# Attention and two expert layers on one core: PSUM in one-bank tiles, the first pair's key-value group in two parts, first loads on two queues

## The chip, the cores and the metric

The kernel runs on one core of a Trainium2 chip. The metric is the device time of one execution in microseconds (us); the number that counts is the median over several executions. The core has TensorE (PE: matmuls, with weight loads shown apart as PEld), VectorE (DVE), ScalarE (ACT), GpSimd (POOL) and SyncE (SP, which here issues loads and stores). Each engine works through its own instructions in the order in which the program was written out, and waits where an instruction needs something that another engine hasn't delivered.

## The reference, cut to what matters

Three stages follow each other, all in float32:

```python
def phi(x):                                   # q, k: (4, 8, 576, 64), w_phi: (64, 128)
    proj = np.einsum('bhsd,df->bhsf', x, w_phi)
    proj = proj - np.max(np.abs(proj), axis=-1, keepdims=True)
    return np.concatenate([np.exp(proj), np.exp(-proj)], axis=-1)
q_p, k_p = (phi(q), phi(k))
kv = np.einsum('bhsf,bhsd->bhfd', k_p, v)
z = np.sum(k_p, axis=2)
num = np.einsum('bhsf,bhfd->bhsd', q_p, kv)
den = np.einsum('bhsf,bhf->bhs', q_p, z)[..., None] + 1e-06
x = num / den                                 # then 2304 tokens of 512 features
...
e_idx = np.argmax(x @ w_gate, axis=1)         # 8 experts, one for each token
h = np.maximum(x[mask] @ w1[e], 0.0)
out[mask] = gate_w[mask, None] * eom[mask, e, None] * (h @ w2[e])
...
xn = x / np.sqrt(np.mean(x * x, axis=-1, keepdims=True) + 1e-06) * rms_g
g = xn @ w_gate
return (g * (1.0 / (1.0 + np.exp(-g))) * (xn @ w_val)) @ w_out     # 512 -> 1536 -> 512
```

## The kernel before, in words

**Attention** (`attn`, L358) runs over four batches, and in each over four pairs of heads. Of the 576 rows of a head 512 are handled in four chunks of 128; the 64 left over of all eight heads are packed into one more pass, the leftovers `"L"`. For each of them a load (L367, L373) brings rows of `k` or `q`, PE transposes them (L400), ACT copies them (L403), PE projects them (L410) into a tile `pp` of two banks of PSUM, and DVE takes the maximum (L414) and subtracts it (L416), which gives `d`. For keys ACT makes the exponentials `e` (L465), PE multiplies them with `v` in groups of five matmuls for each head, four chunks and the leftovers (L474 to L480), and the result goes by way of `ks` (L481, L486) into `kv` (L490). For queries PE transposes `d`, ACT takes exponentials (L433), PE multiplies with `kv` (L533), DVE divides (L440 to L444) into `x`, PE transposes it, and ACT and DVE write it as two parts that add up to it (L545, L547) into `xh`.

**The first expert layer** (`gate`, L582, and `moe`, L698) follows for each batch. From the leftovers alone an expert is guessed for the whole batch (`guess`, L553), whose number, `star` (L576), is read by SP so that the expert's weights can be loaded early (L711); ACT and DVE split them into two parts (L712, L713). Then come sixteen groups of twelve matmuls for the first product (`mm1`, L682; each is read by ACT, L729, and DVE, L731, which write `h`) and eight groups of 24 for the second (`mm2`, L691; read by DVE, L743, into `y`). Tokens that would have needed another expert are handled by `general` (L899) afterwards.

**The second layer** (`unit`, L846) takes the tokens in six units of 384. In a unit, for each of twelve pieces of the hidden size, PE makes a gate and a value product (L860, twelve matmuls each, written out in two halves of six), ACT applies the activation to the first (L866), DVE multiplies it with the second (L868), ACT and DVE split the product in two parts (L870, L871), and PE multiplies them with the output weights (L878). The weights come in a packed form that ACT and DVE decode from `raw` (L776 to L789): half of the gate and value weights during the last expert stage, the rest during unit 0. The next unit's input is normalised (`prep`, L802) beside.

**The order** of all this is not written by hand. A planner (`Graph`, L42) keeps the ready tasks of each engine, gives each a cost (`dur`) and a priority, and writes out in each step the task that could start first by its own clock; tasks take buffers from slots with names (`pa`, `pp`, `ph`, `pgv`, `po`, `pms` for PSUM). The waits between engines are put in below the planner, by the tile: an instruction waits for those written out before it that used the same tile in a conflicting way.

**PSUM** has eight banks. `psum` (L299) makes one pool of two tiles of two banks, `pq0` and `pq1`, and four of one bank. The two-bank tiles serve the projections. After nine of them `pq1` leaves that duty (`halve`, L308) and its halves become two more slots `ph` for the experts' groups, three in all. In the second layer `pgv` is a one-bank tile, both halves of `pq1` and one half of `pq0`:

```python
        self.ps = one + [t[:, i] for t in self.two[::-1] for i in range(2)]
...
    g.slot("pgv", kk.ps[3:7])
```

## Time and profile before

| | |
|---|---|
| Time, median of 3 runs | 957.31 us (956.15 to 957.85) |
| The profiled execution: its own time | 959.13 us |
| Its span | 957.5 us, 14539 instructions |
| PE busy | 914.5 us (96%) |
| weight loads busy | 835.9 us (87%) |
| DVE busy | 433.9 us (45%) |
| ACT busy | 337.4 us (35%) |
| moved by DMA | 74.60 MB, mean 78 GB/s |

The stretches give the busy time of each engine in a part of the span and the clock that PE was granted, as a share of 2.4 GHz; the waits give the idle time of an engine by what ended it; the timeline has instructions in order of time, neighbours of one kind in one row, with the idle time of their engine ahead of them in brackets. A float32 matmul stands in the trace as two records in attention and as one in the expert layers. The batches of attention and of the first expert layer lie interleaved up to about 364 us, the last batch's expert stage fills the time up to 483, then come the border and unit 0 of the second layer (to about 576), and units 1 to 5.

### The profile page before, as it was taken

The page shows a single profiled execution, that of the slowest core. Times are in us where ns is not written, and L with a number is a line of the kernel's source. Part 1 is how long each engine was busy: PE and PEld are TensorE (multiplying, and loading weights), DVE is VectorE, ACT ScalarE, POOL GpSimd, SP SyncE. Part 2 cuts the span into 40 slices and gives each one's busy share as a digit, 9 for nine tenths or more (in the row PEclk, how much of TensorE's full clock was granted, in tenths as well). Part 3 has the DMA queues.
Part 4 walks back from the last instruction along what each step waited for, and adds up shares of the span by engine and source line. Part 5 has one row for each costly group of instructions (what it writes and reads, how often), then busy time and mean ns, then how long its engine had stood idle before and what let it go on. Part 6 is the DMA issues. An engine that isn't in the chain of part 4 may idle for free. (4 is left out here: it accounts for less than half of the span.)

```text
span 957.5 us, 14539 instructions
## 1 busy us (share of the span) xinstructions
PE 914.5 (96%) x6044; PEld 835.9 (87%) x6045; DVE 433.9 (45%) x826; ACT 337.4 (35%) x588; POOL 3.2 (0%) x23
## 2 busy tenths in 40 slices
PE   7988999999999998999989799999999999999998
PEld 5677799789889997898988789999999998999997
DVE  4454565556444547884248882322323133132111
ACT  4343435534433325543145551322223123122111
POOL 1000000000000000000000000000000000000000
PEclk9997999999999999999999989999999999999999
DMA  5313513421511146673145440002001002000000
GB/s 147 105 56 109 139 47 117 143 62 45 180 56 55 49 159 200 181 231 102 48 135 156 148 139 34 1 1 67 1 1 66 1 1 67 1 1 34 1 1 34
DMA packets 84984, 74.60 MB, mean 78 GB/s; under 512 B 30256, under 2 KB 78512, under 8 KB 84400
## 3 DMA queue, kind: packets, MB, share of 16 engines
q1 hardware_dynamic: 84912, 73.60, 25.2%
q8 instruction: 50, 0.82, 0.4%
q14 instruction: 22, 0.18, 0.1%
HBM read 54.63 MB, written 18.96 MB: 77 GB/s over the span
## 5 line engine op out<-in xcount | busy, mean ns | idle before, releaser
L860 PE MATMUL pq<-xn,wgv 128*128 128x384 f32 x1296 | 240.0, 338 | 12.3 <-DVE sil L868 12.3
L860 PEld LDWEIGHTS pq<-xn,wgv 128*128 128x128 f32 x1296 | 227.1, 189 | 18.5 <-DVE sil L868 9.2
L878 PE MATMUL ps<-wo,a 128*128 128x512 f32 x648 | 160.5, 392 | 0.0
L868 DVE TENSOR_TENSOR sil<-pq,sil 128x384 f32<-128x384 f32 x71 | 39.6, 557 | 223.9 <-PE pq L860 223.9
L878 PEld LDWEIGHTS ps<-wo,a 128*128 128x128 f32 x648 | 120.7, 188 | 22.0 <-DVE a L871 0.2
L860 PE MATMUL ps<-xn,wgv 128*128 128x384 f32 x432 | 81.2, 335 | 2.5 <-PEq L914 2.5
L860 PEld LDWEIGHTS ps<-xn,wgv 128*128 128x128 f32 x432 | 75.9, 188 | 5.3 <-issue 2.7
L682 PE MATMUL pq<-xh,w 128*128 128x288 f32 x492 | 73.3, 300 | 7.4 <-DVE h L731 7.1
L691 PE MATMUL pq<-h,w 128*128 128x288 f32 x528 | 76.5, 298 | 2.8 <-DVE y L743 2.2
L870 ACT CAST a<-sil 128x384 fp32r<-128x384 f32 x72 | 36.8, 512 | 118.7 <-DVE sil L868 118.7
L682 PEld LDWEIGHTS pq<-xh,w 128*128 128x128 f32 x492 | 66.4, 188 | 10.7 <-DVE h L731 7.5
L691 PEld LDWEIGHTS pq<-h,w 128*128 128x128 f32 x528 | 71.3, 188 | 4.4 <-DVE y L743 3.1
L209 PE MATMUL ps<-kv,qp 128*128 128x65 f32 x512 | 69.2, 276 | 5.7 <-DVE x L444 4.5
L209 PEld LDWEIGHTS ps<-kv,qp 128*128 128x128 f32 x512 | 67.6, 201 | 7.8 <-DVE x L444 4.9
L414 DVE TENSOR_REDUCE m<-pq 128x8 f32<-128x1024 f32 x36 | 43.9, 1223 | 49.6 <-PE pq L410 45.9
L209 PE MATMUL ps<-e,v 128*65 128x256 f32 x256 | 63.2, 389 | 0.7 <-ACT e L465 0.7
L871 DVE TENSOR_TENSOR a<-sil,a 128x384 fp32r<-128x384 f32 x72 | 39.9, 555 | 28.8 <-ACT a L870 28.4
L209 PEld LDWEIGHTS ps<-e,v 128*65 128x65 f32 x256 | 35.0, 142 | 19.3 <-issue 1.8
L712 ACT CAST w<-wr 128x1024 fp32r<-128x1024 f32 x32 | 33.5, 1047 | 45.6 <-PE pq L691 18.5
L713 DVE TENSOR_TENSOR w<-wr,w 128x1024 fp32r<-128x1024 f32 x32 | 39.2, 1224 | 20.5 <-ACT w L712 19.8
L866 ACT ACTIVATE sil<-ps 128x384 f32<-128x384 f32 x35 | 17.2, 491 | 85.6 <-PE ps L860 85.6
L433 ACT ACTIVATE qp<-ps 128x512 f32<-128x512 f32 x64 | 34.7, 598 | 33.6 <-PE ps L209 30.1
(141 smaller groups left out, 985.7 us busy)
## 6 DMA issues: line engine op xcount, KB each, us to landing
wr<-in_moe_w SPq DMA_DIRECT2D x32, 512.0 KB, 3.7
xdr<-xh SPq DMA_DIRECT2D x4, 2304.0 KB, 9.4
raw<-in_moe_w_gate SPq DMA_DIRECT2D x12, 512.0 KB, 3.5
raw<-in_moe_w_val SPq DMA_DIRECT2D x12, 512.0 KB, 4.2
raw<-in_moe_w_out SPq DMA_DIRECT2D x12, 512.0 KB, 3.7
yu<-ydr SPq DMA_DIRECT2D x6, 768.0 KB, 4.9
qk<-in_k SPq DMA_DIRECT2D x16, 256.0 KB, 3.5
v<-in_v SPq DMA_DIRECT2D x32, 128.0 KB, 2.6
```

The lines of the kernel that those rows point to most:

```text
L209: f()
L414: g.t("DVE", dve(1024), lambda: nc.vector.tensor_reduce(out=m.ap, in_=pv(), axis=AX.X, op=ALU.max, apply_absolute_value=True), r=[pp], w=[ ...
L433: g.t("ACT", act(512), lambda f=f: nc.scalar.activation(qp.ap[:, f].rearrange("p c t -> p (c t)"), pd.ap, AF.Exp, scale=1.0 - 2.0 * f), r= ...
L682: self.nc.tensor.matmul(ph[:, 0:HS], lhsT=wv[:, a, c, fs], rhs=xh[:, x, c, cs], start=(c == 0 and i == 0), stop=(c == NC - 1 and i == 2))
L691: self.nc.tensor.matmul(ph[:, 0:HS], lhsT=wv[:, a, f], rhs=hs[f][:, x, cs], start=(f == 0 and i == 0), stop=(f == 7 and i == 2))
L712: g.t("ACT", act(1024, False), lambda: nc.scalar.copy(w.ap[:, 0], wr.ap), r=[wr], w=[w], prio=pr - AHEAD)
L713: g.t("DVE", dve(1024), lambda: nc.vector.tensor_tensor(out=w.ap[:, 1], in0=wr.ap, in1=w.ap[:, 0], op=ALU.subtract), r=[wr], rw=[w], prio= ...
L860: nc.tensor.matmul(ps.ap[:, 0:UT], lhsT=w[:, i, a, c], rhs=xn[c].ap[:, x], start=(c == 0 and n == 0), stop=(c == NC - 1 and n == 2))
L868: g.t("DVE", dve(UT), lambda sil=sil, ps=pgv[1]: nc.vector.tensor_tensor(out=sil.ap, in0=ps.ap[:, 0:UT], in1=sil.ap, op=ALU.mult), r=[pgv[ ...
L870: g.t("ACT", act(UT, False), lambda sil=sil, a=a: nc.scalar.copy(a.ap[:, 0], sil.ap), r=[sil], w=[a], prio=pr)
L871: g.t("DVE", dve(UT), lambda sil=sil, a=a: nc.vector.tensor_tensor(out=a.ap[:, 1], in0=sil.ap, in1=a.ap[:, 0], op=ALU.subtract), r=[sil], ...
L878: nc.tensor.matmul(po[t].ap, lhsT=a.ap[:, x, ts], rhs=w[:, y], start=(f == 0 and n == 0), stop=(f == NF - 1 and n == 2))
```

## The change

1. *PSUM.* The pool has four one-bank tiles and one of two banks; the second of two banks has a pool of its own, which is closed after nine projections and opened again as two one-bank tiles `ph`. At the border to the second layer all these pools are closed and opened as eight one-bank tiles `pz`, of which the second layer's slots are made.
2. *The first pair's group.* In each batch, the eight matmuls with the first pair's own chunks are a task of its own, ahead of the leftovers; the two with the leftovers follow in the same bank when these are ready.
3. *The first loads.* `w_phi` and, in the first batch, the leftovers of `k` and `q` are issued by ACT, ahead of everything else on its queue, instead of by SP.

The core of the diff (the copies of `psum`'s slots into `general` and `build` are left out: they take the new tiles by other names):

```diff
@@ Graph.free_slot
-                self.slots[rule[2]].extend((f[0], n + i, a) for i, a in enumerate(rule[3]))
+                self.slots[rule[2]].extend((f[0], n + i, a) for i, a in enumerate(rule[3]()))
@@ K.attn_consts, K.psum, K.halve
-            self.g.t("SP", 0.6, lambda i=i: nc.sync.dma_start(self.wraw[i * D:(i + 1) * D], self.w_phi),
-                     w=[self.cBw], prio=0.5, nbytes=1 << 15)
+            self.g.t("ACT", 0.6, lambda i=i: nc.scalar.dma_start(self.wraw[i * D:(i + 1) * D], self.w_phi),
+                     w=[self.cBw], prio=-2, nbytes=1 << 15)
-        ps = self.pool(ctx, "ps", space=PSUM)
-        self.two = [ps.tile([P, 2, 512], F32, name=f"pq{i}") for i in range(2)]
-        one = [ps.tile([P, 512], F32, name=f"ps{i}") for i in range(4)]
-        self.ps = one + [t[:, i] for t in self.two[::-1] for i in range(2)]
+        self.banks, self.pair = ExitStack(), ExitStack()
+        p = self.pool(self.banks, "ps", space=PSUM)
+        one = [p.tile([P, 512], F32, name=f"ps{i}") for i in range(4)]
+        two = [p.tile([P, 2, 512], F32, name="pq0"),
+               self.pool(self.pair, "pq", space=PSUM).tile([P, 2, 512], F32, name="pq1")]
+        self.last = two[0]
         self.g.slot("pa", one[0:3])
-        self.g.slot("pp", self.two)
+        self.g.slot("pp", two)
         self.g.slot("ph", one[3:4])
+        self.g.retire("pp", 9, two[1], "ph", self.halve)
     def halve(self):
-        self.g.retire("pp", 9, self.two[1], "ph", [self.two[1][:, i] for i in range(2)])
+        self.pair.close()
+        p = self.pool(self.pair, "ph", space=PSUM)
+        return [p.tile([P, 512], F32, name=f"ph{i}") for i in range(2)]
+    def psum2(self, ctx):
+        self.pair.close()
+        self.banks.close()
+        p = self.pool(ctx, "pz", space=PSUM)
+        return [p.tile([P, 512], F32, name=f"pz{i}") for i in range(8)]
@@ K.attn
+        eng, dma = ("ACT", nc.scalar.dma_start) if b == 0 else ("SP", nc.sync.dma_start)
...
-                    g.t("SP", 0.6, lambda i=i, j=j, m=m: nc.sync.dma_start(
+                    g.t(eng, 0.6, lambda i=i, j=j, m=m: dma(
                         t.ap[j * 64:(j + 1) * 64, i], m[b, j::2, MAIN:S].rearrange("h t d -> t h d")),
-                        w=[t], prio=np_, nbytes=LEFT * H * D * 2)
+                        w=[t], prio=-1 if b == 0 else np_, nbytes=LEFT * H * D * 2)
...
+        def kv_part(j, pr, e, v, np_, pk, part):
+            def fn():
+                ops = [(v.ap[:, j, c], e.ap[:, at(j, c)]) if c < NC else
+                       (vl.ap[:, j, pr], el.ap[:, (pr % 2) * 2 + pr // 2]) for c in part]
+                return [partial(nc.tensor.matmul, pk.ap[0:D + 1, j * 256:(j + 1) * 256], lhsT=v_,
+                                rhs=e_.rearrange("p f e -> p (f e)"), start=(c == 0 and (pr > 0 or j == 0)), stop=(c == NC), skip_group_check=True)
+                        for c, (v_, e_) in zip(part, ops)]
+            g.t("PE", len(part) * 0.431, fn, r=([e, v] if 0 in part else []) + ([el, vl] if NC in part else []),
+                rw=[pk], prio=np_, kind="pass", steps=len(part))
...
             if el is None:
+                first = g.buf("pa")
+                for j in range(2):
+                    kv_part(j, *ready[0], first, range(NC))
                 continue
             for pr, e, v, np_ in ready:
-                pk, ks, pz = g.buf("pa"), g.buf("ks"), g.buf("pa")
+                pk, ks, pz = first if pr == 0 else g.buf("pa"), g.buf("ks"), g.buf("pa")
                 for j in range(2):
...
+                    kv_part(j, pr, e, v, np_, pk, (NC,) if pr == 0 else range(NC + 1))
@@ build
-    g.slot("po", kk.ps[0:3])
-    g.slot("pgv", kk.ps[3:7])
-    g.slot("pms", kk.ps[7:8])
+    g.slot("po", banks[0:3])
+    g.slot("pgv", banks[3:7])
+    g.slot("pms", banks[7:8])
```

The planner writes out the whole attention and first expert layer in another order with it. From the last expert stage on PE, DVE and ACT have the same instructions in the same order in both. Three places show what moves.

SP, the first loads, before, from the fifth on (ahead of these are one of `w_phi`, one of `k` and two of `v`; `graw` are the two gates' weights, `vl` the leftovers of `v`):

```order
L296 DMA wraw<-in_w_phi 64x128
L373 DMA qk_143<-in_k 64x4x64 x2
L373 DMA qk_143<-in_q 64x4x64 x2
L388 DMA vl_149<-in_v 64x4x64 x2
L367 DMA qk_144<-in_k 128x2x256
L382 DMA v_147<-in_v 128x4x64 x2
L367 DMA qk_145<-in_k 128x2x256
L382 DMA v_148<-in_v 128x4x64 x2
L367 DMA qk_142<-in_k 128x2x256
L367 DMA qk_143<-in_q 128x2x256
L272 DMA graw<-in_moe_w_gate 128x4x8
L272 DMA graw<-in_moe_w_output_gate 128x4x8
```

and in the change, from the first on (L272 is the same line; L382, L397 and L403 are L367, L382 and L388 of before):

```order
L272 DMA graw<-in_moe_w_gate 128x4x8
L382 DMA qk_145<-in_k 128x2x256
L397 DMA v_149<-in_v 128x4x64 x2
L403 DMA vl_152<-in_v 64x4x64 x2
L382 DMA qk_147<-in_k 128x2x256
L397 DMA v_150<-in_v 128x4x64 x2
L382 DMA qk_148<-in_k 128x2x256
L397 DMA v_151<-in_v 128x4x64 x2
L382 DMA qk_145<-in_k 128x2x256
L272 DMA graw<-in_moe_w_output_gate 128x4x8
```

The two loads of `w_phi` and the four of the leftovers are gone from the front, and both gates' loads stand further ahead; ahead of the second of them stood twenty loads, and now stand thirteen.

DVE, around the first expert choice (`star`), before:

```order
L576 TENSOR_SCALAR star<-m_0_134 1x1
L578 TENSOR_SCALAR os_136<-g_1_131,m_0_134 128x8
L416 TENSOR_TENSOR d_154<-pq_79,m_157 128x1024
L440 TENSOR_SCALAR r_185<-ps_81 128x4
L442 RECIPROCAL r_185<-r_185 128x4
L444 TENSOR_TENSOR x_182<-ps_81,r_185 128x4x64
L713 TENSOR_TENSOR w_111<-wr_109,w_111 128x1024
L440 TENSOR_SCALAR r_184<-ps_81 128x4
L442 RECIPROCAL r_184<-r_184 128x4
L444 TENSOR_TENSOR x_181<-ps_81,r_184 128x4x64
L547 TENSOR_TENSOR xh_99<-ps_82,xh_99 128x512
L713 TENSOR_TENSOR w_112<-wr_110,w_112 128x1024
```

and in the change:

```order
L599 TENSOR_SCALAR star<-m_0_137 1x1
L601 TENSOR_SCALAR os_139<-g_1_134,m_0_137 128x8
L455 TENSOR_SCALAR r_187<-ps_81 128x4
L457 RECIPROCAL r_187<-r_187 128x4
L459 TENSOR_TENSOR x_185<-ps_81,r_187 128x4x64
L570 TENSOR_TENSOR xh_102<-ps_79,xh_102 128x512
L736 TENSOR_TENSOR w_114<-wr_112,w_114 128x1024
L455 TENSOR_SCALAR r_188<-ps_81 128x4
L736 TENSOR_TENSOR w_115<-wr_113,w_115 128x1024
L457 RECIPROCAL r_188<-r_188 128x4
L459 TENSOR_TENSOR x_185<-ps_81,r_188 128x4x64
```

The splits of the first two pieces of the expert's weights (L713, now L736) stand with one small row between them, where four rows, an `x` and an `xh` among them, lay between them before.

PE, the first products of the second layer, with the semaphores that a row waits for, before (`pq_80` is one tile of two banks, and holds the value product of piece 0 and the gate product of piece 1):

```order
L860 MATMUL pq_80<-xn_2963,wgv_2977 128x384 x3
L860 MATMUL pq_80<-xn_2964,wgv_2977 128x384 x3
L860 MATMUL pq_80<-xn_2965,wgv_2977 128x384 x3
L860 MATMUL pq_80<-xn_2966,wgv_2977 128x384 x3
L860 MATMUL pq_80<-xn_2963,wgv_2978 128x384 x3
L860 MATMUL pq_80<-xn_2964,wgv_2978 128x384 x3
L860 MATMUL pq_80<-xn_2965,wgv_2978 128x384 [waits DVE_49]
L860 MATMUL pq_80<-xn_2965,wgv_2978 128x384 x2
L860 MATMUL pq_80<-xn_2966,wgv_2978 128x384 x3
```

and in the change, from the same product on:

```order
L883 MATMUL pz_4739<-xn_2972,wgv_2986 128x384 [waits PE_49]
L883 MATMUL pz_4739<-xn_2972,wgv_2986 128x384 x2
L883 MATMUL pz_4739<-xn_2973,wgv_2986 128x384 x3
L883 MATMUL pz_4739<-xn_2974,wgv_2986 128x384 x3
L883 MATMUL pz_4739<-xn_2975,wgv_2986 128x384 x3
L883 MATMUL pz_4740<-xn_2972,wgv_2987 128x384 x3
L883 MATMUL pz_4740<-xn_2973,wgv_2987 128x384 x3
L883 MATMUL pz_4740<-xn_2974,wgv_2987 128x384 x3
L883 MATMUL pz_4740<-xn_2975,wgv_2987 128x384 x3
L883 MATMUL pz_4741<-xn_2972,wgv_2987 128x384 x3
```

The wait for DVE in the middle of the gate product is gone.

## Rows read from the trace of the kernel before

**Rows 1.** stretches: length, busy PE, PEld, DVE, ACT, POOL; PEclk, DMA share, GB/s.
```profile
0.00:40.00 40.00, 32.20 (x244) 24.31 (x247) 15.77 (x18) 17.30 (x25) 3.21 (x23) 1.00 0.50 125
60.00:100.00 40.00, 34.44 (x244) 29.91 (x245) 18.02 (x40) 18.30 (x31) 0.00 (x0) 0.87 0.41 132
100.00:360.00 260.00, 259.94 (x2176) 233.03 (x2175) 138.00 (x315) 107.62 (x190) 0.00 (x0) 1.00 0.30 92
360.00:486.00 126.00, 113.51 (x820) 108.97 (x819) 75.68 (x134) 47.34 (x81) 0.00 (x0) 1.00 0.48 147
486.00:560.00 74.00, 65.06 (x336) 60.02 (x335) 60.68 (x109) 40.88 (x69) 0.00 (x0) 0.95 0.53 160
560.00:950.00 390.00, 386.68 (x2039) 361.33 (x2038) 111.45 (x188) 98.23 (x179) 0.00 (x0) 1.00 0.06 20
```

**Rows 2.** stretches, the two at half clock.
```profile
40.00:44.00 4.00, 4.00 (x31) 3.05 (x28) 2.96 (x3) 1.31 (x3) 0.00 (x0) 0.57 0.69 222
74.00:85.00 11.00, 10.63 (x47) 9.57 (x48) 4.36 (x10) 2.90 (x5) 0.00 (x0) 0.53 0.30 95
```

**Rows 3.** waits, whole span: who, for whom, total us, times, longest.
```profile
PE pq L860 <- DVE sil L868: 12.3, 10, 6.2
PE pq L682 <- DVE h L731: 7.1, 9, 1.8
PE pq L691 <- DVE y L743: 2.2, 4, 0.6
PE ps L209 <- DVE x L444: 4.5, 2, 3.5
PE ps L400 <- DMA qk<-in_k: 3.3, 3, 1.9
PE ps L400 <- DMA qk<-in_q: 1.2, 2, 0.7
PE ps L209 <- ACT e L465: 0.7, 1, 0.7
```

**Rows 4.** timeline, unit 1 of the second layer: start, duration, what, [idle before].
```profile
654.42 0.56 DVE L868 TENSOR_TENSOR sil<-pq,sil 128x384 f32<-128x384 f32 x1 [1.40 <-PE pq L860]
655.03 3.39 PE L860 MATMUL pq<-xn,wgv 128*128 128x384 f32 x18 [0.65 <-DVE sil L868]
```

**Rows 5.** waits from 475 to 560.
```profile
DVE sil L868 <- PE pq L860: 11.3, 4, 7.5
```

**Rows 6.** timeline of PE, unit 0 of the second layer.
```profile
552.59 3.78 PE L860 MATMUL pq<-xn,wgv 128*128 128x384 f32 x12 [6.19 <-DVE sil L868]
```

**Rows 7.** timeline, last expert stage.
```profile
380.32 1.97 DVE L819 TENSOR_TENSOR xn<-yu,xn 128x384 fp32r<-128x384 f32 x4 [1.29 <-ACT xn L818]
382.20 0.45 DVE L731 SCALAR_TENSOR_TENSOR h<-pq,h 128x288 fp32r<-128x288 f32 x1
382.71 1.86 PE L682 MATMUL pq<-xh,w 128*128 128x288 f32 x12 [1.69 <-DVE h L731]
```

**Rows 8.** timeline, the start.
```profile
0.92 0.59 SPq L296 DMA_DIRECT2D wraw<-in_w_phi  x1
13.74 0.50 SPq L272 DMA_DIRECT2D graw<-in_moe_w_output_gate  x1
17.78 0.20 DVE L277 CAST wgt<-graw 128x64 fp32r<-128x64 f32 x1 [4.15 <-DMA graw<-in_moe_w_output_gate]
```

**Rows 9.** timeline around the first expert choice.
```profile
54.59 2.00 PE L209 MATMUL ps<-kv,qp 128*128 128x65 f32 x16
56.91 0.66 PE L209 MATMUL ps<-ident,d 128*128 128x128 f32 x4
57.65 1.08 ACT L433 ACTIVATE qp<-ps 128x512 f32<-128x512 f32 x2 [0.27 <-PE ps L209]
64.67 0.13 DVE L576 TENSOR_SCALAR star<-m 1x1 int32<-1x1 f32 x1
71.27 1.04 ACT L712 CAST w<-wr 128x1024 fp32r<-128x1024 f32 x1 [2.32 <-DMA wr<-in_moe_w]
```

More of the change, by code (lines that the diff above doesn't have):

```diff
@@ L295, in attn_consts, with psum @@
         for i in range(2):
-            self.g.t("SP", 0.6, lambda i=i: nc.sync.dma_start(self.wraw[i * D:(i + 1) * D], self.w_phi),
-                     w=[self.cBw], prio=0.5, nbytes=1 << 15)
-    def psum(self, ctx):
-        ps = self.pool(ctx, "ps", space=PSUM)
-        self.two = [ps.tile([P, 2, 512], F32, name=f"pq{i}") for i in range(2)]
-        one = [ps.tile([P, 512], F32, name=f"ps{i}") for i in range(4)]
-        self.ps = one + [t[:, i] for t in self.two[::-1] for i in range(2)]
+            self.g.t("ACT", 0.6, lambda i=i: nc.scalar.dma_start(self.wraw[i * D:(i + 1) * D], self.w_phi),
+                     w=[self.cBw], prio=-2, nbytes=1 << 15)
+    def psum(self):
+        self.banks, self.pair = ExitStack(), ExitStack()
[4 more added lines that the diff above has]
+        self.last = two[0]
         self.g.slot("pa", one[0:3])
-        self.g.slot("pp", self.two)
+        self.g.slot("pp", two)
         self.g.slot("ph", one[3:4])
+        self.g.retire("pp", 9, two[1], "ph", self.halve)
     def halve(self):
-        self.g.retire("pp", 9, self.two[1], "ph", [self.two[1][:, i] for i in range(2)])
+        self.pair.close()
[6 more added lines that the diff above has]
+        return [p.tile([P, 512], F32, name=f"pz{i}") for i in range(8)]
     def warm(self, n):
@@ L469, in attn @@
             if el is None:
+                first = g.buf("pa")
+                for j in range(2):
+                    kv_part(j, *ready[0], first, range(NC))
                 continue
             for pr, e, v, np_ in ready:
-                pk, ks, pz = g.buf("pa"), g.buf("ks"), g.buf("pa")
+                pk, ks, pz = first if pr == 0 else g.buf("pa"), g.buf("ks"), g.buf("pa")
                 for j in range(2):
-                    def kvm(j=j, pr=pr, e=e, v=v, pk=pk):
-                        ops = [(v.ap[:, j, c], e.ap[:, at(j, c)]) for c in range(NC)]
-                        ops.append((vl.ap[:, j, pr], el.ap[:, (pr % 2) * 2 + pr // 2]))
-                        return [partial(nc.tensor.matmul, pk.ap[0:D + 1, j * 256:(j + 1) * 256], lhsT=v_,
-                                        rhs=e_.rearrange("p f e -> p (f e)"), start=(n == 0), stop=(n == NC))
-                                for n, (v_, e_) in enumerate(ops)]
-                    g.t("PE", 5 * 0.431, kvm, r=[e, v, el, vl], rw=[pk], prio=np_, kind="pass", steps=5)
+                    kv_part(j, pr, e, v, np_, pk, (NC,) if pr == 0 else range(NC + 1))
                 g.t("ACT", act(512), lambda pk=pk, ks=ks: nc.scalar.copy(ks.ap, pk.ap[0:D + 1]),
@@ L954, in general @@
                 self.use_phase2(g3)
-                g3.slot("pms", self.ps[7:8])
+                g3.slot("pms", [self.last[:, 1]])
                 g3.slot("xn", xn0)
@@ L974, in build @@
     kk.consts(ctx)
-    kk.psum(ctx)
-    kk.halve()
+    kk.psum()
     moe = ExitStack()
@@ L1000, in build @@
         g.slot("xn", kk.xn)
-        g.slot("pms", kk.ps[6:7])
+        g.slot("pms", [kk.last[:, 0]])
         for f in range(NPRE):
@@ L1010, in build @@
     moe.close()
+    banks = kk.psum2(ctx)
     p = kk.pool(ctx, "p2", side="right")
```

## The prediction

> **What bounds the kernel now.** I read the stretches first, then the waits, then the timeline around the longest of them. The profiled execution took 959.13 us for a span of 957.5; the median of the runs is 957.31, 1.8 below it. TensorE (PE) works in order and is busy nearly throughout, so the end moves only by what PE idles and by what it runs at half clock. The stretches show where that is [rows 1]: 7.8 us idle in 0:40 (40 − 32.20), 5.6 in 60:100, 0.06 in 100:360, 12.5 in 360:486, 8.9 in 486:560, 3.3 in 560:950. Two stretches at half clock (1.2 instead of 2.4 GHz) come on top [rows 2]: a granted 0.57 over 40:44, 0.53 over 74:85, after PE had idled. Full speed would have done the work of those 15 us in 4 × 0.57 + 11 × 0.53 = 8.1, so they cost 1.7 and 5.1.
>
> The waits say who holds PE [rows 3]: a gate or value product (L860) waits for VectorE's (DVE's) multiplication of the gated value, 12.3 us in 10 waits; the expert's first product (L682) for DVE's `h`, 7.1 in 9; its second (L691) for DVE's `y`, 2.2 in 4. All three are tiles named `pq`, the two-bank ones.
>
> **The change part by part.**
>
> *The five later units of the second layer: 3.3 us.* In the order as printed, six of the twelve matmuls of the next gate product stand ahead of DVE's multiplication in the same two-bank tile, and the rest wait for it. The timeline shows it [rows 4]: DVE idles 1.40 until PE is done with those six, multiplies for 0.56, and PE idles 0.65. The wait falls once in a unit, where no output product lies between the two. With one tile for one bank the printed order of the change has the same instructions and no such wait. Five of the ten waits belong to units 1 to 5 and are all the idle that PE has in 560:950 (390 − 386.68). Nothing is late next: the first output product needs its operand only after two products that still lie ahead of it. Gain 5 × 0.65 = 3.3, bounds 2.6 and 3.3.
>
> *The first unit: 4.5 us.* Here DVE sets the pace, since it decodes weights: 60.68 of 74 us busy [rows 1]. DVE's own waits for PE at the multiplication are 11.3 in 4 [rows 5]. The first, 7.5, is the border between the layers, and only the six matmuls in it are false: 6 of 18 records that take 3.39 [rows 4], 1.1. The other three, 3.8 together, are all false: the product they read had ended before. So DVE can come up to 4.9 earlier to the multiplication for which PE idles 6.19 ahead of 552.59 [rows 6]. That wait is real (PE writes the very bank that DVE reads) and stays, shorter from its far end: PE's resumption moves with DVE. The four short waits of PE ahead of it, about 0.7 each, only lengthen it. What is late next is the raw weights, loaded into two buffers that DVE frees; I take 4.5 off, with 0 (loads bind at once) and 6.5 (4.9, and 1.6 for the half clock after 552 avoided) as bounds.
>
> *The last expert stage: 8.0 us.* `h` and `y` waits are 7.1 + 2.2 = 9.3 [rows 3]. The order of this stage is the same in both kernels. With two halves in one tile, a group that overwrites one half waits for the reading of the other half as well, which comes a group of twelve matmuls, 1.86 us [rows 7], later. With three separate banks a group waits only for the reading two groups back. One of the waits is not false: the 1.69 before 382.71 [rows 7] waits for an `h` that DVE reaches only at 382.20, after four subtractions of `xn` of 1.97 together, which waited 1.29 for ScalarE. Following DVE from the first wait, it gets there some 2 to 3 us earlier, PE 3.4, so about 1.3 stays. 9.3 − 1.3 = 8.0; bounds 4.5 (half of the waits for `h` are DVE's lateness too: 2.2 + 3.6 − 1.3) and 9.3 (all).
>
> *The start: 4.1 us.* SyncE (SP) issues loads in a row from 0.92 on: 20 of them lie ahead of the output gate's weights, issued at 13.74 and landed at 17.78 [rows 8], so one takes 0.64. DVE stands on that load, 4.15 idle, with the third group's reduction behind it. The change has 13 ahead, so issue at about 0.92 + 13 × 0.64 = 9.2, landing 4.0 later at 13.3. The leftover keys now come behind it on DVE and take back part of the 4.5 us; PE meanwhile has the first pair's eight products, which used to need the leftovers. The waits of PE in 0:40 that go are those for `in_k` 3.3, `in_q` 1.2 and `e` 0.7 [rows 3], 5.2 together, and the half clock at 40 that followed one of them, 1.7. New ones: the leftovers' projection now stands behind the third pair's transposes, whose load is tenth, issued at 0.92 + 9 × 0.64 = 6.7, landed 4.0 later at 10.7; following the rows one by one, PE has nothing from about 8.8, 1.9 idle, then 0.4 for the next load and 0.5 around the first `ks` (estimates). 5.2 + 1.7 − 2.8 = 4.1. ScalarE's (ACT's) issues have no row; at SP's 0.64 the six take 3.8 and end at 4.7, which I take to leave its first copy in time. Bounds −4 (each takes twice as long, and the first copy is late by that) and 8 (all idle of 0:40).
>
> The Trainium skill ("DMA: Bandwidth & Descriptors", section "Issuing engines are not separate DMA queues") says that transfers started by several engines run on the same 16 DMA engines, so that a second queue saves only the time of issuing. By that the start could gain at most the six issues moved, 3.8 us, and the sum would be 19.6 (as an estimate, by SP's durations). The trace has the DMA engines at a 0.50 share in 0:40, so they aren't full on average, and agrees that the issues are what stands in line.
>
> *Around the first expert choice: 0.* The choice (L576) is ready at 64.67, its weights are cast at 71.27, 6.6 later [rows 9], and PE idles 4.5 in two waits, 3.5 the longer [rows 3], for `x` that stands behind DVE's split of them; then comes the half clock, 5.1. In the change both casts stand together on ACT, ahead of the exponentials of the next product, and both splits on DVE with one small row between. From the choice: 6.6, two casts of 1.04, two exponentials of 1.08, some 9.8; PE has about 6.0 of work until then: 0.7 left of one product, another of 2.00, and five groups of four transposes at 0.66 [rows 9]. 3.8 idle against 4.5 now: even, the half clock included. Bounds −4 (the loads land that much later) and +8.6 (no idle, no half clock).
>
> *Nothing:* matmuls, evacuations and bytes are the same in number; pools reopened at the border add waits for engines already done there.
>
> **Sum.** 3.3 + 4.5 + 8.0 + 4.1 + 0 = 19.9. From 959.13 that gives 939.2; as the median lies 1.8 lower, 937.4.
>
> **The rivals.**
>
> *DVE sets the pace in both crowded places.* For it: DVE's 60.68 of 74, and 75.68 of 126 with the decoding in its front part. Against: DVE's idle there is itself partly waiting for PE. Then the stage gives 4.5, the first unit 0: 3.3 + 4.5 + 4.1 = 11.9, so 945.4. Chance 0.17.
>
> *The clock holds.* If PE's idle after the expert choice comes out short, the 5.1 of half clock go too: 932.3. For it: the idle is a difference of two sums, each good to a microsecond or two. Chance 0.13.
>
> *Only the tiles miss* (the waits come back as others on DVE or ACT, the change doesn't do what it says): 4.1 remain, 953.2. Against: the printed waits are gone. Chance 0.04.
>
> *Slower: the weight splits stall every batch.* Splits in DVE's and ACT's queues ahead of rows that PE needs cost the first batch 3.5 and 5.1. Batches 1 to 3 have the same rows, and now another order. Lost there in each, 8.6 × 3 = 25.8 less 19.9: 963.2. It decides from 6.6 lost per batch. Against: in 100:360 PE idles 0.06 [rows 1], since the previous batch's expert products lie between, as they still do. Chance 0.05.
>
> **How the numbers follow.** The forecast has 0.60, 930 to 944 by its own bounds; 0.01 is left to no change. A measurement here tells some 0.2%, 1.9 us, from none. All cases but the last and that one are below 955.4: faster 0.93, same 0.02 (a little of the tiles' rival is put there), slower 0.05. The range goes from below the clock's case to past DVE's: 927 to 950.
>
> **What would show it.** PE's waits for `sil` in units 1 to 5 gone; the 6.19 ahead of 552.59 about 4 shorter; waits for `h` one or two, for `y` none; the second layer's first product some 12 earlier. Wrong: new waits of PE inside 100:360; the output gate's load landing after 16; a half clock at other places.

## The result and the profile after

| | before | after |
|---|---|---|
| Time, median | 957.57 us (956.15 to 957.85, 4 runs) | 932.84 us (932.26 to 935.70, 4 runs) |
| The profiled execution: its own time, its span | 959.13, 957.5 us | 935.70, 934.1 us |
| PE busy | 914.5 us (96%) | 912.5 us (98%) |

The ratio is 0.9751 with a 95% interval of 0.9728 to 0.9773: 24.7 us faster, where 19.9 were forecast. 932.84 lies inside the range (927 to 950), and nearer to the rival in which the clock holds (932.3) than to the forecast (937.4); but the clock did not hold, and the second half of this text is about that.

Both kernels have the same instructions from the last expert stage on, so the two spans can be cut at the same products: at the first product of that stage, at the first of the second layer, and at two products of unit 0. Before, the columns as in [rows 1]:

```profile
0.00:367.61 367.61, 353.13 (x2890) 309.57 (x2892) 189.76 (x407) 153.17 (x262) 3.21 (x23) 0.98 0.34 104
367.61:485.70 118.09, 106.15 (x769) 102.39 (x769) 70.37 (x120) 43.85 (x77) 0.00 (x0) 1.00 0.45 135
485.70:552.59 66.89, 57.95 (x306) 53.59 (x306) 53.98 (x97) 36.45 (x62) 0.00 (x0) 0.97 0.52 156
...
575.98:957.50 381.52, 373.89 (x1971) 349.08 (x1969) 101.35 (x170) 90.08 (x164) 0.00 (x0) 1.00 0.06 19
```

and after, cut at the same products:

```profile
0.00:364.58 364.58, 356.92 (x2890) 315.57 (x2891) 191.43 (x408) 153.54 (x262) 3.22 (x23) 0.96 0.34 104
364.58:469.88 105.30, 102.56 (x769) 101.90 (x769) 69.44 (x119) 45.38 (x78) 0.00 (x0) 1.00 0.49 151
469.88:533.64 63.76, 56.89 (x305) 53.80 (x306) 54.18 (x97) 35.11 (x61) 0.00 (x0) 0.98 0.54 165
...
557.28:934.10 376.82, 372.50 (x1971) 349.25 (x1969) 101.16 (x170) 90.13 (x164) 0.00 (x0) 1.00 0.06 20
```

The first number behind the stretch is its length. By the differences, everything ahead of the last expert stage gained 3.0, the stage 12.8, unit 0 up to its long wait 3.1, units 1 to 5 4.7; the 23 us between the last two cuts lost 0.25. Together 23.4, the difference of the spans. In the stage and in units 1 to 5 two columns shrink, not one: idle (11.94 to 2.74 and 7.63 to 4.32), and also PE's busy time for the same number of records (106.15 to 102.56, 373.89 to 372.50).

The waits of PE over the whole span of after (who, for whom, total us, times, longest), which answer to [rows 3]:

```profile
PE pz L883 <- DVE sil L891: 6.9, 1, 6.9
PE ps L415 <- DMA qk<-in_k: 2.6, 2, 1.8
PE pz L883 <- PEq L937: 1.9, 1, 1.9
...
PE ps L583 <- ACT qp L448: 1.0, 1, 1.0
PE ps L209 <- ACT qp L448: 1.0, 1, 1.0
PE ph L705 <- DVE h L754: 0.4, 1, 0.4
PE ps L705 <- DVE h L754: 0.4, 1, 0.4
```

Of ten waits for `sil` one is left, of nine for `h` two, of four for `y` none. These are the printed waits that the forecast called false. The one left for `sil` went from 6.19 [rows 6] to 6.87 in this profile; in the two later profiles of the changed kernel it is 5.75 and 6.12.

### The profile page after: what moved, and what is told of

It is laid out like the page before. It is cut to its first block, busy times and chain, and to the rows that moved or that the text cites. A ratio compares the mean times of both kernels' runs of the same rounds, so it can differ in the third digit from the quotient of the medians.

```text
span 934.1 us, 14538 instructions
## 1 busy us (share of the span) xinstructions
PE 912.5 (98%) x6044; PEld 842.3 (90%) x6045; DVE 434.7 (47%) x826; ACT 338.1 (36%) x588; POOL 3.2 (0%) x23
## 5 line engine op out<-in xcount | busy, mean ns | idle before, releaser
L883 PE MATMUL pz<-xn,wgv 128*128 128x384 f32 x1728 | 313.6, 337 | 8.8 <-DVE sil L891 6.9
L883 PEld LDWEIGHTS pz<-xn,wgv 128*128 128x128 f32 x1728 | 303.2, 189 | 14.8 <-issue 9.3
L901 PE MATMUL pz<-wo,a 128*128 128x512 f32 x648 | 160.4, 392 | 0.0
L901 PEld LDWEIGHTS pz<-wo,a 128*128 128x128 f32 x648 | 120.9, 188 | 21.9
L714 PE MATMUL ph<-h,w 128*128 128x288 f32 x528 | 75.9, 297 | 0.0
L705 PE MATMUL ph<-xh,w 128*128 128x288 f32 x492 | 71.5, 298 | 0.4 <-DVE h L754 0.4
L714 PEld LDWEIGHTS ph<-h,w 128*128 128x128 f32 x528 | 71.2, 188 | 0.4
L705 PEld LDWEIGHTS ph<-xh,w 128*128 128x128 f32 x492 | 66.6, 188 | 1.3 <-DVE h L754 0.7
L736 DVE TENSOR_TENSOR w<-wr,w 128x1024 fp32r<-128x1024 f32 x32 | 39.2, 1224 | 23.1 <-ACT w L735 22.0
L735 ACT CAST w<-wr 128x1024 fp32r<-128x1024 f32 x32 | 33.5, 1049 | 38.3 <-PE ph L705 11.4
L425 PE MATMUL pq<-wraw,x 64*128 64x128 f32 x576 | 43.2, 289 | 1.2 <-ACT x L418 1.2
L431 DVE TENSOR_TENSOR d<-pq,m 128x1024 f32<-128x1024 f32 x36 | 43.9, 1220 | 0.7
```

What stands on the lines that cost most here:

```text
L425: nc.tensor.matmul(pp.ap[:, hf, k * FE:(k + 1) * FE], lhsT=xt.ap[r, k], rhs=self.wraw[r], start=True, stop=True)
L431: g.t("DVE", dve(1024), lambda: nc.vector.tensor_tensor(out=d.ap.rearrange("p h k f -> p (h k) f"), in0=pv(), in1=m.ap.unsqueeze(2).to_bro ...
L705: self.nc.tensor.matmul(ph[:, 0:HS], lhsT=wv[:, a, c, fs], rhs=xh[:, x, c, cs], start=(c == 0 and i == 0), stop=(c == NC - 1 and i == 2))
L714: self.nc.tensor.matmul(ph[:, 0:HS], lhsT=wv[:, a, f], rhs=hs[f][:, x, cs], start=(f == 0 and i == 0), stop=(f == 7 and i == 2))
L736: g.t("DVE", dve(1024), lambda: nc.vector.tensor_tensor(out=w.ap[:, 1], in0=wr.ap, in1=w.ap[:, 0], op=ALU.subtract), r=[wr], rw=[w], prio= ...
L883: nc.tensor.matmul(ps.ap[:, 0:UT], lhsT=w[:, i, a, c], rhs=xn[c].ap[:, x], start=(c == 0 and n == 0), stop=(c == NC - 1 and n == 2))
```

## The experiments

Twelve runs follow: ten other kernels, and the changed kernel twice more. Where a text says when the last expert stage begins, that is the length of everything ahead of it; this, the stage, unit 0 up to its long wait, and the rest are read from each profiled execution with the cuts above.

### The change taken apart

**The tiles alone.** PSUM as in the change, the first pair's group whole again, and all first loads SyncE's (the lines that go, against the changed kernel):

```diff
-        eng, dma = ("ACT", nc.scalar.dma_start) if b == 0 else ("SP", nc.sync.dma_start)
-                first = g.buf("pa")
-                for j in range(2):
-                    kv_part(j, *ready[0], first, range(NC))
```

> Only the PSUM part of the change; the first pair's group is whole again and all first loads are SyncE's. Theory: the tiles carry the stage (12.8 us between the first product of the last expert stage and the first of the second layer), unit 0 (3.1) and the later units (4.5), 20.4 together, and the attention part before it stays within 2 us of the kernel before: 957.6 - 20.4 = 937.2. Rival: the gain of the stage came from the new order of attention ahead of it, then the stage gives the forecast's 8.0 or less and the time is 942 or more.

Measured: 934.71 (ratio 0.9766, 0.9746 to 0.9787), 23.0 us off. Everything ahead of the stage, the stage and unit 0:

```profile
0.00:363.63 363.63, 353.80 (x2890) 312.45 (x2891) 190.91 (x408) 153.29 (x262) 3.21 (x23) 0.98 0.35 105
363.63:468.24 104.61, 102.29 (x770) 101.86 (x769) 69.15 (x119) 45.46 (x78) 0.00 (x0) 1.00 0.50 152
468.24:531.84 63.60, 56.86 (x306) 53.77 (x306) 53.92 (x97) 35.44 (x61) 0.00 (x0) 0.98 0.55 166
```

The stage is as short as in the whole change, under an order of attention that has neither the split nor the new loads. The rival falls: the stage's gain is the tiles'. The theory missed elsewhere: the stage begins at 363.63, 4.0 earlier than before where at most 2 were expected, and no later than in the profile of the whole change (364.58). So the 3.0 that the whole change gained ahead of the stage can't be put down to the split and the loads. Why the tiles alone gained there is open; the kernel below that has the tiles in the second layer alone, with the attention of before, began its stage at 365.34, so 2.3 of such a difference can come from one execution to the next.

**The start alone.** The kernel before, with the split group and with the six loads on ScalarE (the diff shows the split; the loads are as in the change):

```diff
+                first = g.buf("pa")
+                for j in range(2):
+                    kv_part(j, *ready[0], first, range(NC))
```

> Only the first pair's group in two parts and the six first loads on ScalarE's queue; PSUM as before. Theory: what the tiles don't carry, 24.7 - 20.4 = 4.3 us: 953.3, with the last expert stage within 1 us of its 118.1 before. Rival: the start only trades idle time for half clock, 956 to 959.

Measured: 955.65, ratio 0.9986 (0.9962 to 1.0011), which can't be told from no change. The twelve single times lie in two heaps, six at 952.6 to 953.5 with a mean granted clock of 0.988 to 0.991 and six at 957.8 to 962.2 with 0.978 to 0.984. In the profiled one (953.01) the stage began at 361.36 and took 117.64, as before. The theory holds for one heap and the rival for the other; the section on the clock takes this up.

**The second layer's tiles alone.** Attention and the first expert layer with the two-bank tiles of before, `pz` at the border:

```diff
+        self.banks.close()
+        p = self.pool(ctx, "pz", space=PSUM)
+        return [p.tile([P, 512], F32, name=f"pz{i}") for i in range(8)]
```

> One-bank tiles in the second layer alone; everything ahead of the border as before. Theory: 3.1 (unit 0) + 4.5 (units 1 to 5) = 7.6, so 950.0, and a unit lasts 0.94 us less though the trace showed 0.65 idle in it. Rival (only the idle shown counts, and unit 0 was carried by a VectorE that came freer out of the stage): 3.3, so 954.3.

Measured: 948.21 (0.9902, 0.9884 to 0.9921), 9.5 us off; in its profile 8.4 lie behind the border (unit 0 62.84 against 66.89, the rest 400.56 against 404.91). The stage and unit 0:

```profile
365.34:483.20 117.86, 106.20 (x770) 102.45 (x769) 70.36 (x120) 45.16 (x78) 0.00 (x0) 1.00 0.44 135
483.20:546.04 62.84, 56.86 (x305) 53.78 (x306) 53.93 (x97) 35.28 (x61) 0.00 (x0) 0.98 0.54 166
```

The stage keeps its 118. So the 13 us that the tiles gain in the stage come from the halves `ph` becoming tiles of their own, and unit 0's doesn't need a VectorE that comes freer out of the stage. The rival falls here too.

**The loads without the split.**

```diff
-                    kv_part(j, pr, e, v, np_, pk, (NC,) if pr == 0 else range(NC + 1))
+                    g.t("PE", 5 * 0.431, kvm, r=[e, v, el, vl], rw=[pk], prio=np_, kind="pass", steps=5)
```

> The whole change but for the first pair's group, which is one task of ten matmuls again. Theory: the first loads carry the gain of the start, 4.3, and the split none: 933. Rival: without the split TensorE has nothing ahead of the leftovers' key exponentials and the first two waits for loads come back: 937 as with the tiles alone.

Measured: 933.96 (0.9757, 0.9736 to 0.9779). It lies between the two expectations, and the intervals of this run, the tiles alone and the whole change overlap: the split by itself can't be told from none, and by 934.71 and 933.96 neither can the loads. That stays open.

### What a wait costs

The stage's waits of [rows 3] sum to 9.3, yet it lost 12.8. The timeline of PE in the stage before shows the rest:

```profile
379.28 1.74 PE L682 MATMUL ps<-xh,w 128*128 128x288 f32 x12
...
384.41 1.74 PE L682 MATMUL ps<-xh,w 128*128 128x288 f32 x12
385.99 1.80 PE L682 MATMUL pq<-xh,w 128*128 128x288 f32 x12
```

A group that follows another begins 1.58 after it (384.41 to 385.99) though its record lasts 1.74: the records overlap by 0.16. Ahead of the wait at 382.71 [rows 7] there is no such overlap (379.28 + 1.74 + 1.69 = 382.71), and the group behind the wait takes 1.70 to the next start instead of 1.58. So that wait cost its 1.69 and 0.16 + 0.12 = 0.28 more. The sums say the same: in the stage some 12 waits went with 3.59 us of busy time, 0.30 each, in units 1 to 5 five with 1.39, 0.28 each. A unit's false wait was 0.94, not 0.65. The second layer's tiles alone, with the same gain behind unit 0 (4.4), repeat it. The Trainium skill ("Perfetto Trace Analysis", section "Tensor Engine Instruction (MATMUL, LD_WEIGHTS)") says that TensorE's ends are estimated by the profiler rather than observed; these rows fit that, since an idle time that begins at such an end comes out short of what the wait took, but they don't tell an estimated end from an overlap that is really lost.

### Unit 0: VectorE's pace

VectorE's waits in unit 0, from the border to the long wait, before:

```profile
DVE ww L779 <- DMA raw<-in_moe_w_val: 1.9, 2, 1.1
```

and after:

```profile
DVE sil L891 <- PE pz L883: 5.9, 1, 5.9
DVE ww L802 <- DMA raw<-in_moe_w_gate: 1.9, 2, 1.2
DVE ww L802 <- DMA raw<-in_moe_w_val: 1.2, 2, 0.9
...
DVE ww L802 <- DMA raw<-in_moe_w_out: 0.6, 2, 0.4
```

Its waits for PE went from 11.3 [rows 5] to 5.9, the 4.9 of the forecast and a little more, and 1.8 of that came back as waits for raw weights (1.9 to 3.7). Busy 54.2, 4.5 of the 5.9 (the rest of that wait lies ahead of the border), the 3.7, and 1.1 for ScalarE's casts: 63.5 of unit 0's 63.8, so VectorE's own time fills it from end to end. Two runs went after the rest.

**Without the loads** (the raw weights of unit 0 aren't loaded, and the decoding works on what lies in the buffers):

```diff
-        g.t("SP", 0.5, lambda: nc.sync.dma_start(src[0](raw.ap), src[1]), w=[raw], prio=prio, nbytes=1 << 19)
+        g.t("SP", 0.5, lambda: None if hasattr(self, "wout") else nc.sync.dma_start(src[0](raw.ap), src[1]),
+            w=[raw], prio=prio, nbytes=1 << 19)
```

> The changed kernel without the loads of raw weights in unit 0 (the decoding works on what is left in the buffers, so unit 0's later weights are not the reference's). Theory: VectorE's waits for raw, 3.7 us in unit 0, are part of the chain that sets TensorE's wait of 6.87: unit 0 takes 63.8 - 3.7 = 60.1, the whole 929. Rival: VectorE's own work is the bound and the waits lie where it would have waited for TensorE or ScalarE anyway: unit 0 above 62.5, the whole above 931.5.

Measured: 932.65, 2.2 below the changed kernel beside it (934.85), which is within the spread of the two (930.31 to 934.22, and 929.72 to 938.52); unit 0 61.58 against 64.21 there. VectorE's waits in it:

```profile
DVE sil L892 <- PE pz L884: 6.1, 1, 6.1
DVE wgv L813 <- ACT wgv L812: 2.9, 3, 1.3
```

The two profiles differ in one more thing, the products right behind the border, first here, then in the changed kernel beside it:

```profile
468.64 8.58 PE L884 MATMUL pz<-xn,wgv 128*128 128x384 f32 x48 [2.11 <-PEq L938]
```

```profile
463.22 10.16 PE L883 MATMUL pz<-xn,wgv 128*128 128x384 f32 x48 [1.98 <-PEq L937]
```

There the granted clock was 0.66 over the first 5 us, here 1.00. The profiles with loads that were at full speed there have unit 0 at 63.76 (the first of after) and 62.77 (the fills into a free bank, below). So the result lies between the two: the loads cost 1.2 to 2.2 of the 3.7, and behind them stands ScalarE's cast, whose waits rose from 1.1 to 3.3.

**Two loads ahead of the border.**

```diff
+        early = [g.buf("raw", True) for _ in range(2)]
+        for f, t in enumerate(early):
+            g.t("SP", 0.5, lambda f=f, t=t: nc.sync.dma_start(t.ap, kk.mo[f * P:(f + 1) * P]),
+                w=[t], prio=2100 + f, nbytes=1 << 19)
```

> The changed kernel with the first two pieces of the output weights loaded as the last loads ahead of the border, so that their decoding steps (some 2.5 us of VectorE) and the next loads come before VectorE's idle 5.93 at the border ends. Theory: unit 0 is set by VectorE and its loads, so it shortens by 2.5 to 4: 59.8 to 61.3, the whole about 929.5. Rival: the two raw buffers bind as before and TensorE's wait only moves: unit 0 within 1 us of 63.8.

Measured: 939.96 (0.9810, 0.9786 to 0.9834), 5.1 slower than the changed kernel beside it; unit 0 took 68.54, and PE's wait in it grew to 9.18. VectorE's waits there:

```profile
DVE wo L813 <- ACT wo L812: 6.7, 1, 6.7
DVE ww L803 <- DMA raw<-in_moe_w_out: 5.3, 4, 1.8
```

The expectation was wrong. The planner, told that the raw weights are there, wrote other work out in another order: VectorE's first instruction behind the border waits for a cast that stands on ScalarE behind the first activation, which waits for PE's first product. So the idle at the border stayed (6.7; 7.6 in the changed kernel beside it, 5.9 in its first profile). VectorE's waits in unit 0 sum to 13.6 against 11.5 beside it, and 56.8 of work against 53.8 now stands ahead of the multiplication for which PE waits. It is worse than the rival, which had the wait only move.

### The clock

The changed kernel was run again as a measure, and its profile fell upon an execution at the lower end (929.72).

> The changed kernel once more, as the measure for the three runs beside it: 932.8. Its half-clock stretches in attention fall at other places than in its first profile (the kernel with the tiles in the second layer alone has the attention of before and showed that), while the last expert stage (105.3 us), unit 0 (63.8) and the rest (400.5) repeat within 0.5 us.

Measured: 934.85 (929.72 to 938.52). Three stretches of this execution, then the same of the first profile of after:

```profile
8.00:20.00 12.00, 9.46 (x67) 7.11 (x66) 7.58 (x8) 5.78 (x9) 0.00 (x0) 0.86 0.81 222
48.00:64.00 16.00, 14.51 (x99) 13.54 (x95) 8.29 (x24) 5.97 (x11) 0.00 (x0) 0.79 0.19 66
64.00:82.00 18.00, 16.25 (x148) 14.68 (x149) 11.14 (x23) 9.14 (x16) 0.00 (x0) 1.00 0.49 155
```

```profile
8.00:20.00 12.00, 9.38 (x67) 7.12 (x66) 7.51 (x8) 5.40 (x8) 0.00 (x0) 0.86 0.78 207
48.00:64.00 16.00, 14.97 (x94) 14.34 (x91) 7.59 (x22) 5.30 (x10) 0.00 (x0) 0.68 0.20 66
64.00:82.00 18.00, 16.86 (x99) 16.25 (x99) 6.67 (x19) 5.50 (x10) 0.00 (x0) 0.62 0.24 75
```

The same program had a granted clock of 1.00 in 64:82 once and of 0.62 (long at 0.50, 1.2 GHz) the other time, and did 148 matmul records there for 99. The stage began at 357.98 against 364.58; stage, unit 0 and the rest repeat within 0.5. PE idles 8.0 ahead of the stage in the one and 7.7 in the other, so it is busy time that differs: the spread between these two is the half clock in the first 85 us. The kernel's six times also fall in the order of their mean clock (0.989 for 929.72, 0.979 for 938.52). Before the fall in 48:64 PE had had no wait since 12 but one of 1.00, here in the first profile of after:

```profile
51.48 0.40 PE L583 MATMUL ps<-wgt,xh 128*64 128x8 f32 x4 [1.00 <-ACT qp L448]
```

**Filling the waits, first try.** Matmuls on a constant ahead of the instructions that wait:

```diff
+    def fill(self, n, ap):
+        for i in range(n):
+            self.nc.tensor.matmul(ap[:, 0:P], lhsT=self.mean, rhs=self.mean, start=True, stop=True)
...
+                    if b == 0 and pr == 2 and j == 0:
+                        self.fill(20, pn.ap)
```

> The changed kernel with matmuls that no one reads put where TensorE waits in attention: 5 ahead of the first projection, 4 and 8 ahead of the third and fourth transposes, 4 ahead of the first expert choice's product, 20 ahead of the first product of the third pair; all into the bank that the waiting instruction overwrites. Theory: the clock falls because TensorE idled; with the idle filled it stays at full speed in 0:100, worth 1.7 + 6.8 of its first profile and about 1.3 at the choice, less what other executions of it had already: 925 to 928. Rival: the half clock comes whether TensorE idles or not, then the fills run at half clock and overshoot the waits: 934 to 942.

Measured: 933.01 (932.54 to 936.67) against 934.85 beside it: between the two. Full speed held until about 62 us, then fell. The timeline of PE shows why it gained so little:

```profile
63.60 7.22 PE L335 MATMUL ps<-mean 128*128 128x128 f32 x40 [2.38 <-ACT qp L456]
```

The fill's bank was still being read, so the fill waited for what the product would have waited for, and then ran 7.2 us for nothing.

**Filling into a free bank**, the single-bank tile that the experts use only later, with 2, 4, 8, 4 and 10 matmuls (against the run before it):

```diff
-            self.nc.tensor.matmul(ap[:, 0:P], lhsT=self.mean, rhs=self.mean, start=True, stop=True)
+            self.nc.tensor.matmul(self.spare[:, 0:P], lhsT=self.mean, rhs=self.mean, start=True, stop=True)
...
+        self.last, self.spare = two[0], one[3]
```

> The same fills as the run that put them into the waiting instruction's bank, but into a bank that nothing uses until the first expert product, so that they wait for nothing, and shorter: 2, 4, 8, 4 and 10 matmuls. Theory: the clock falls because TensorE idled, and the last run lost its gain to 20 matmuls that stood behind a bank's reader and then ran for 7.2 us after it; now attention is at full speed throughout and the last expert stage begins at about 357 (357.98 in the execution of the changed kernel that had the least half clock): 927 to 929, and the executions lie closer together than the changed kernel's 929.7 to 938.5. Rival: a half clock comes in 50:80 anyway: 932 to 936.

> The changed kernel beside the two runs with fills, on the same chip: 932 to 935.

Measured: 928.31 (925.59 to 929.67; 0.9704, 0.9679 to 0.9729) against 934.68 (932.90 to 935.42; 0.9768, 0.9746 to 0.9790) of the changed kernel on the same chip. The fill and the three stretches:

```profile
60.78 2.45 PE L335 MATMUL ps<-mean 128*128 128x128 f32 x20
```

```profile
8.00:20.00 12.00, 10.79 (x92) 8.80 (x91) 7.24 (x8) 5.39 (x8) 0.00 (x0) 1.00 0.84 227
48.00:64.00 16.00, 15.37 (x129) 13.99 (x127) 9.79 (x26) 6.71 (x11) 0.00 (x0) 1.00 0.26 83
64.00:82.00 18.00, 17.12 (x156) 15.30 (x156) 10.35 (x21) 9.11 (x16) 0.00 (x0) 1.00 0.52 173
```

The granted clock is 1.00 over the whole of 0:100, and the stage begins at 356.43. The five profiles that have the change's attention without fills stand at 0.68 to 0.79 over 48:64; the three with fills into a free bank, the two below among them, at 1.00. So PE's idle was what brought the half clock, and 28 matmuls that nobody reads are worth 6.4 us. They don't hold it in every execution alike: the mean clock of this one is 0.996, that of two of the other four 0.991 (929.46 and 929.67).

**A fill in unit 0 as well**, 24 matmuls into the eighth bank ahead of the product of the 6.9 wait:

```diff
+                    if u == 0 and f == 10 and i == 0 and part[0] == 0:
+                        self.fill(24)
```

> As the run before it, and 24 matmuls into the second layer's eighth bank ahead of the product for which TensorE idles 6.9 in unit 0. Theory: the half clock after that wait (531 to 537) goes, worth about 1.6: 1 to 2 below the run before it. Rival: the wait is VectorE's, so nothing but TensorE's own speed after it changes, and the fills end after it: no gain, up to 1 slower.

Measured: 927.39 (925.36 to 927.62; 0.9690, 0.9669 to 0.9712), the fastest kernel of this study, 30 us under before; its interval and the one of the run without this fill overlap. The half clock after the wait went, and this is what came of it, first without the fill, then with it:

```profile
462.27 8.59 PE L895 MATMUL pz<-xn,wgv 128*128 128x384 f32 x48 [2.44 <-PEq L949]
...
525.04 4.18 PE L895 MATMUL pz<-xn,wgv 128*128 128x384 f32 x12 [5.88 <-DVE sil L903]
...
531.47 2.76 PE L895 MATMUL pz<-xn,wgv 128*128 128x384 f32 x15
```

```profile
461.51 10.14 PE L897 MATMUL pz<-xn,wgv 128*128 128x384 f32 x48 [2.08 <-PEq L951]
...
525.57 2.32 PE L897 MATMUL pz<-xn,wgv 128*128 128x384 f32 x12 [0.26 <-DVE sil L905]
...
529.72 1.89 PE L915 MATMUL pz<-wo,a 128*128 128x512 f32 x7 [1.37 <-DVE a L908]
531.44 2.76 PE L897 MATMUL pz<-xn,wgv 128*128 128x384 f32 x15
```

The product takes 2.32 instead of 4.18, then PE waits for VectorE's `a`, and is at 531.4 either way. That favours the rival, by which a faster PE is worth nothing here, but the pair doesn't settle it: with the fill the border came 0.76 earlier, and the 48 products behind it ran partly at half clock (10.14 for 8.59). From the border the last product shown stands at 69.9 with the fill and at 69.2 without. The two later profiles of the changed kernel, which also have that half clock, reach it at 70.3 and 70.6, so by them the fill is worth 0.4 to 0.7. The theory's 1 to 2 is not shown.

**The start once more, with the clock held.** The tiles alone, with fills ahead of their eight longest waits in attention:

```diff
+FILL = {("projection", 0): 2, ("projection", 1): 3, ("transposes", 3): 7, ("transposes", 10): 9, ("keys", 2): 4,
+        ("queries", 2): 4, ("queries", 4): 4, ("queries", 5): 12}
```

> The kernel with the tiles alone (no split group, first loads on SyncE), with matmuls that no one reads ahead of its eight longest waits in attention, into the bank that nothing uses until the first expert product, so that neither of the two starts has half clock. Theory (the forecast's term): the split and the loads save 4.1 of idle at the start, and nothing at the choice; the last expert stage then begins at 356.4 + 4.1 = 360.5 and the time is 928.3 + 4.1 = 432 above 500, that is 932.4. Rival: the start gains nothing once the clock is held: 356 to 358 and 928 to 930.

Measured: 931.25 (929.93 to 933.64; 0.9733, 0.9716 to 0.9749). The granted clock is 1.00 over the whole of 0:100 here too, and the stage's first product stands at

```profile
360.35 1.85 PE L706 MATMUL ps<-xh,w 128*128 128x288 f32 x12
```

and with the split and the loads (the fills into a free bank) at

```profile
356.43 1.85 PE L717 MATMUL ps<-xh,w 128*128 128x288 f32 x12
```

3.9 us earlier. In the times it is 2.9, from two chips, between theory and rival. The 3.9 can't be set beside the forecast's 4.1, since 1.7 of that was a half clock which neither of these kernels has; what remains of the forecast is 5.2 − 2.8 = 2.4. And PE idles 5.1 ahead of the stage in both; what differs is the fills, 11.4 us for 45 matmuls here and 7.2 for 28 there. How long either kernel would have waited at full speed in these places without fills no run shows, so what part of the 3.9 is the split's and the loads' stays open. In the changed kernel as it stands no gain of theirs can be told from none: its three medians are 932.84, 934.85 and 934.68, that of the tiles alone 934.71.

## Why the prediction was right

The direction and the cause were right: false waits on two-bank tiles carried the change (23.0 by the tiles alone, where the whole change took 24.7, 22.5 and 22.4 off the kernel beside it). By its steps, with the profiled pair:

| step | forecast | measured |
|---|---|---|
| units 1 to 5 | 3.3 (2.6 to 3.3) | 4.7 |
| unit 0 | 4.5 (0 to 6.5) | 2.9 (3.1 − 0.25) |
| last expert stage, with the border | 8.0 (4.5 to 9.3) | 12.8 |
| start, and first expert choice | 4.1 and 0 | 3.0, but 4.0 with the tiles alone; 3.9 between the two kernels with fills, its share open |
| sum | 19.9 | 23.4 |

- *Units 1 to 5, the last expert stage.* The mechanism was right and the size was off, by one mistake: "Gain 5 × 0.65 = 3.3" and "9.3 (all)" took the idle that a wait shows for the whole that it costs. It costs 0.28 to 0.30 more. Of the stage's 12.8, 9.2 are idle and 3.6 this. Both upper bounds were too low for the same reason. The residue was forecast as 1.3 and is 0.85, in two short waits, and the border's wait fell by 0.56, which the forecast had left out.
- *Unit 0.* DVE's waits for PE shrank by 5.4 (4.9 forecast), and what was named as late next, the raw weights, took back 1.8. The value taken, 4.5, was too near to the free end. "The 6.19 ahead of 552.59 about 4 shorter" was wrong: it stayed about as long (6.87, 5.75 and 6.12 in three profiles). In the first of them PE arrives there 3.8 earlier and VectorE only 3.1. The working had it ("the four short waits ... only lengthen it"); the line on what would show it didn't follow the working.
- *The start.* The output gate's load was issued at 10.61 and landed at 14.83, for 9.2 and 13.3 forecast: the loads ahead of it took some 0.75 each on SP instead of 0.64. ScalarE's six issues ended at 4.9 (4.7 forecast), but its table load now stands behind them, so its first copy begins at 6.25 instead of 5.98:

```profile
3.63 1.30 ACTq L388 DMA_DIRECT2D qk<-in_q  x2
4.96 1.28 ACT L418 ACT_TABLE_LOAD   x1 [4.83 <-issue]
```

PE's idle over 0:40 came out as forecast all the same, 5.2 instead of 7.8, that is 2.6 less for 5.2 − 2.8 = 2.4:

```profile
0.00:40.00 40.00, 34.83 (x238) 26.08 (x240) 13.97 (x17) 16.86 (x24) 3.22 (x23) 0.96 0.49 121
```

What failed is the 1.7 for the half clock: the one at 40 is gone, and one of the same size stands at 8:20 (0.86 of 12 us). So of the 4.1 the runs show the idle, not the clock, and no run shows the whole.

- *The first expert choice.* "3.8 idle against 4.5 now: even, the half clock included" was wrong in kind. PE idles only 2.0 there now, in two waits of 1.00, since it works at half clock through most of the time in which it would have waited; but the half clock then comes a second time. 0.68 over 48:64 and 0.62 over 64:82 stand against the 0.53 over 11 us of [rows 2]. The bound of 8.6 there also counted the longer wait alone; with both, 4.5 and 5.1, it is 9.6.
- *The clock's rival* (932.3) named the right place, and its price of 5.1 was near: with the idle filled the time is 928.3, 6.4 lower. It needed the idle filled, not merely short. That the median fell so near to 932.3 is luck: the clock did not hold, and the 6.2 that the last stage and units 1 to 5 gave beyond the forecast stood in for it.

The Trainium skill ("DMA: Bandwidth & Descriptors", section "Issuing engines are not separate DMA queues") says that a second issuing engine saves only the time of issuing; the prediction's 3.8 was an estimate from that and from SP's durations. No run here shows that bound or breaks it: the loads without the split (933.96) lie 0.75 below the tiles alone (934.71), which can't be told from none.

## What to carry to other kernels

Look for waits between an engine and the reader of another part of the same tile: where dependences are kept by the tile, a buffer shared by two groups needs a tile for each. Count such a wait on TensorE by the distance between starts with and without it, not by the idle that is printed. Where TensorE must wait and its clock falls, matmuls into a bank that nobody uses can be cheaper than the half clock that follows; into a bank with a reader they only queue. And before two profiles are compared in a stretch, its granted clock has to be compared.

## What was not expected of the hardware

Two executions of one program differed by 6.6 us ahead of the last expert stage (364.58 and 357.98) by where the granted clock stood at 0.50. The clock fell after a single wait of 1.00 us (ahead of 51.48 in the first profile of after), with no other in the 35 us before it, while in the profile of the kernel with the free-bank fills, where that wait is filled, it stood at 1.00 up to the long wait of unit 0. And a wait as long did not always bring a fall: behind the border, after waits of 1.89 and 2.44, the first 5 us ran at 1.00 in two profiles, and after 1.98 and 2.08 at 0.66 in two others. What decides there is open.
